# First channel product of six token groups as seven block products for eight, in a DeltaNet and low-rank mixer kernel

## The chip, the core and the metric

The kernel runs on one core of one Trainium2 chip. The metric is the device time of one execution in microseconds; the median of three runs of the kernel before is 591.05 us (590.74 to 592.5). The engines are called as in the profile: PE (TensorE matmuls; PEld is its weight loads), DVE (VectorE), ACT (ScalarE), POOL (GpSimd) and SP (SyncE, which here issues transfers).

## The reference

Four sequences of 768 tokens, eight heads of width 48. A delta-rule recurrence per head gives `x`, and a mixer follows. Its two channel products, `u @ w_ch1` (384 to 1536) and the product with `w_ch2` (1536 to 384), are most of the arithmetic.

```python
for t in range(S):                                   # 768 tokens
    kt, vt, bt = (k_n[:, :, t], v[:, :, t], beta[:, :, t, None])
    y[:, :, t] = np.einsum('bhd,bhde->bhe', q[:, :, t], state)
    v_old = np.einsum('bhde,bhd->bhe', state, kt)
    state = state + bt[:, :, :, None] * np.einsum('bhd,bhe->bhde', kt, vt - v_old)
...
xt = x.transpose(0, 2, 1)                            # x: (4, 768, 384)
h = xt @ U @ V                                       # over the tokens, rank 32
u = x + h.transpose(0, 2, 1)
ch = np.maximum(u @ w_ch1, 0.0) @ w_ch2
return (u + ch).astype(np.float32)
```

All matmuls are fp32. The weights arrive as 64-bit words and are converted on the chip.

## The kernel before

**Recurrence.** Each sequence is cut into 12 chunks of 64 tokens, in two units of six (`UC`); units are numbered 0 to 7. For each unit DVE inverts small triangular blocks by substitution (`blocks`, L790 and L796, a product and a subtraction for each of some 31 columns), PE joins the blocks with 32x32 products (L887 to L908), and `recur` walks the chunks: in the later units a step is a product with the state (L1066), a subtraction on DVE (`w`, L1078), a product (L1090), a copy on ACT (`z`, L1099), a product (L1135) and the new state on DVE (L1147, or L1149 for a sequence's first). Output products (L972, L986) go beside them. All of these use quarters of the array: four 64x64 (or 48x64) matmuls side by side, written in the planner as mode `"Q"`.

**Mixer.** A sequence has three groups of 256 tokens (`NG`), so there are twelve. `front` (L1469 to L1517) makes the transposed tokens `ut`. For groups 1 to 7 `wide` computes the first product as six pairs of output blocks (`PAIRS`, `channels`, L1580): for each pair six full 128x128 matmuls with 256 columns, three blocks of contraction for two blocks of outputs, into one PSUM bank, then one ReLU on ACT (L1545). A full matmul is mode `"F"`. A part whose key is in `PARTED` instead goes as 24 quarter matmuls (`crossed`, L393) over two banks, with a small ACT copy (`swap`, L402) between its halves. `add_up` (L1607) and `last_sum` (L1614) form sums of the hidden activations for the second product (`narrow`, L1695 in full and L393 in quarters), which is done as seven block products for eight over halves of its operands; `gather` (L1620) adds each result to `X`.

The last five groups (`EARLY` and `ordinal`) do the first product otherwise: `first_of` runs 15 block products for 18 (`CHAINS`, `products_of`, L1430), each of four full matmuls with 128 columns. A bank holds a running sum of products; after certain products it is drained: by an ACT copy or ReLU (L1406) where it is the first term of an output block, by a DVE addition or subtraction (L1412) where the block holds something already. `relu_of` (L1442) is the ReLU in SBUF. DVE makes the sums of weights and of tokens (`weight_sums`, `token_sums`, `sum_of`, L1350 and L1355).

**Weights.** `load_weights` brings slices into three places (`room` in `X`, `converted`, and a part of `hs`), and `convert` makes fp32 of them on DVE and ACT (L1229 to L1272), with `exponents` as a second buffer. After the last conversion, `converted` and `exponents` are not used again.

**Order.** The program is recorded through a small planner. Each part is a generator that asks for conditions (`need`) and engine slots (`op`). `ORDER` is a list, written out by hand for each of the five engines, of the parts' keys in the sequence in which their pieces are issued there; the planner follows it. A key such as `99.1` is the second child of part 99; before, `wide` of groups 1 to 12 has the keys 98 to 109 and `first_of` 93 to 97. So what an engine does next is fixed by the list, and it waits there if data are late. When PE goes from quarter to full pieces or back, the planner counts a turn (`TURN`). PSUM has eight banks: `pair` banks for the recurrence and the fronts, `mix` banks 0 and 1 for the mixer of groups 1 to 7, and four more for `CHAINS` once the recurrence is done (`reserve`).

Of the kernel before, what the change touches and what calls it, by code (L numbers as in the profile page):

```python
# [26 lines left out]
def kernel(  # L27
# [68 lines left out]
    def dve(n):  # L96
        return (n + 151) / 960.0
# [30 lines left out]
    def advance(i, value, at):  # L128
# [24 lines left out]
        4.12 32.1 4.13 4*2 4.13 4.14 4 4.15 4 4.14 4.15 79 32.0.0.0 81 32.1.0.0 81*2 40.0 82 98.0*2 39.0  # L153
        39.1 82 98.1 40.1 39.1.0.0 39.0.0.0 98.1 98.2 33.2*2 98.2 98.3*2 98.4 33.4*2 33.2 98.4 33.2 98.5
        33.4*2 33.2*2 98.5 98.7 83 33.2 33.4 33.2 33.4 98.7 33.4*2 98.8 5 5.0 5 40.1.0.0 5 98.8 5.1 5 98.9 5
        98.9 5 5.1 98.9 5 98.9 5.2 5 98.10 5 5.2 5.3 5 99.0 5 99.0 5 5.3 5.4 5 99.0 5 99.0 5.5 5 99.1*2 5
        5.4 99.1*2 5.5 40.0.0.0 5 83 99.2*2 99.3*2 99.4 48.0 99.4 41.2*2 47.0 99.7 47.1 47.0.0.0 47.1.0.0
        41.4*2 99.5*2 48.1 41.2 41.4*2 41.2 99.7 99.8 48.1.0.0 5 99.8 5.6 5 48.0.0.0 5 99.9 5 99.9 5.7 5*2
        99.9 5 5.6 99.9 5.8 5.7 5 99.10 5*2 100.0 5.9 5 100.0 5.8 5 100.0 5 100.0 5.9 5 5.10 5 100.1 5.11 5
        5.10 100.1 5 5.11 100.1*2 84 100.2*2 100.3*2 100.4*2 100.5 100.7 100.5 49.2*2 55.0.0.0 84 55.1.0.0  # L160
        100.7 100.8 49.2 49.4*2 49.2 100.8 84 100.9*2 6 85 100.9 6 100.9 56.0.0.0 56.1.0.0 6 100.10 49.4*2
        6.0 6 101.0*2 85 6.1 6 101.1*2 6 101.1 6 101.1 6.2 6 101.2*2 6.1 6 101.2*2 6 6.3 6.2 101.3 6 101.3 6
        6.4 6.3 6 101.4 6 101.4 6.5 6 101.4 6 101.4 6.4 6 6.5 101.5*2 101.7*2 57.2*2 57.4*2 86 57.4*2 57.2*2
        101.8*2 101.9*2 63.0.0.0 101.10 6 101.10 6 63.1.0.0 102.0*2 86 6.6 6 102.1*2 64.0.0.0 6 6.6 102.2 6
        102.2 6.7 6 102.2*2 6 6.7 102.3 6 102.3 6.8 6 102.3 6 102.3 6.9 6 102.4 6 102.4 6.8 6 102.4 6 102.4
        6.10 6 102.5*2 6.9 6.11 102.5 6 102.5 6.10 6 102.7 6.11 102.7 87 102.7*2 64.1.0.0 87 102.8*2 102.9*2
        102.10 71.0.0.0 103.0*2 71.1.0.0 103.1*2 103.2*2 103.3*2 65.4*2 65.2*2 103.4*2 72.1.0.0 65.2*2
        65.4*2 103.5*2 87 103.7 7 72.0.0.0 7 103.7 7 7.0 103.8*2 7.1 7 103.8*2 7 88 7 103.9*2 7 7.1 7.2 7
        103.10 7 7.2 104.0 7 104.0 7.3 7 104.0*2 7 7.3 7.4 104.1 7 104.1 7 104.1*2 7.5 7 7.4 104.2 7 104.2
        88 104.3*2 7 7.5 73.4*2 73.2*2 104.4*2 104.5 73.4*2 73.2*2 104.5 7 104.7 7 7.6 7 104.7 7 7.7 104.8  # L170
        7.6 7 104.8 7 104.8 7 104.8 7 7.7 7.8 7 104.9 7 7.8 7.9 7 104.9 7 89 7 104.10 7 7.9 7.10 7 7.11 7
        104.10 7 7.10 7.11 79 93.2 93.1 79 89 93.4 93.2 93.1 93.3 93.2 93.3 93.4 93.1 93.5 93.1 93.2 93.1
        94.2 94.3 93.1 90 94.3 94.4 94.2 90 94.1 105.3*2 94.1 94.2 90 94.1 94.5 94.1 94.4 94.2 105.4*2 105.5
        94.1 105.5 94.1 91 105.6 95.2 95.1 91 95.4 106.3 95.2 95.3 95.1 106.3 95.1 95.3 95.4 95.1 95.2
        106.4*2 95.5 95.1 106.5 95.2 96.3 95.1 106.5 96.1 106.6 92 96.4 96.2 96.1 92 96.2 96.4 96.1 96.2
        96.3 96.2 96.1 107.3*2 107.4*2 96.1 96.5 107.5*2 96.1 107.6 97.1 97.4 97.2 97.1 97.3 97.2 97.1
        108.3*2 97.1 97.3 97.2 97.5 108.4*2 97.1 97.2 108.5 97.1 108.5 108.6 97.4 109.3*2 109.4*2 109.5*2
        109.6
# [7 lines left out]
        31.0.0.0*2 31.1.0.0*2 4 33 4 30 4 78.25 4 33*2 4 78.25*2 33*2 78.26 32.0.0.0 78.26 81 33 78.26 81  # L186
        32.1.0.0*2 78.26 33 78.26 33 82 33*2 32.0.0.0 30 33*8 33.4 33.2 78.26.1*3 39.0.0.0 78.27 98.2.1*3
        39.1.0.0 78.26.1 39.0.0.0 30 78.27*4 39.1.0.0 33.2*3 33.4*2 78.27.1 33.4 41 98.5.1*2 78.27.1*2
        98.7.0 98.5.1 78.27.1 38 83 41 98.6 5 98.7.1 41*3 38 98.8.0 5 98.8.1 41*3 5 41 5 41*2 40.1.0.0
        98.9.0 41 98.9.1 5 40.1.0.0 41 98.10.0 5 41*2 5 41 5 41*2 5 41 5 41*15 41.2 5 99.2.1 40.0.0.0 99.2.1  # L190
        38 40.0.0.0 99.2.1 99.7.0 41.4 47.0.0.0*2 47.1.0.0*2 49 99.5.1*3 46 49*2 46 49*2 99.7.1 99.8.0 99.6
        5 48.1.0.0*2 99.8.1 49*2 48.0.0.0 5 48.0.0.0 49 5 49*2 5 49*2 5 99.9.0 49*2 99.9.1 49 99.10.0 5 49 5
        49*2 5 49 5 49*2 5 49 5 49*9 46 49*2 84 49 100.2.1*2 49.2 49.4 55.1.0 55.0.0 100.5.1*2 100.2.1
        100.5.1 100.7.0 84 55.1.0.0 55.0.0.0 55.1.0.0 100.7.1 55.0.0.0 100.6 57 100.8.0 54 100.8.1 56.0.0
        57*4 56.1.0 6 85 100.9.0 56.0.0.0 56.1.0.0 56.0.0.0 6 57 56.1.0.0 100.9.1 100.10.0 57*7 6 57 6 57*2
        6 57*2 6 57*3 101.2.1 57 6 57 6 57*2 6 57 6 57*5 6 54 57*3 57.2 101.2.1 101.7.0 57.4 101.2.1
        101.5.1*3 101.7.1 54 86 101.6 101.8.0 101.8.1 63.0.0 64.0.0 101.9.0 101.9.1 63.1.0 63.0.0.0 6
        63.0.0.0 101.10.1 101.10.0 64.1.0 63.1.0.0*2 65 62 65*2 6 65 64.0.0.0 62 6 64.0.0.0 65*2 6 65*2 6
        65*3 6 65 6 102.2.1 65 6 65 6 65*3 6 102.2.1*2 65 6 65 102.5.1*2 65 62 87 65 102.5.1 102.7.0 65*3
        102.7.1 65 102.8.0 65 102.6 102.8.1 87 65 102.9.0 65 71.0.0 65 102.9.1 102.10.0 64.1.0.0*2 71.1.0  # L200
        65*4 71.1.0.0 65 71.0.0.0 65.4 71.0.0.0 71.1.0.0 65.2 73 72.1.0 72.0.0 70 73*2 72.1.0.0 103.2.1 73
        72.1.0.0 73*3 103.2.1*2 73 103.7.0 103.5.1*2 72.0.0.0 73 7 103.5.1 103.7.1 73 72.0.0.0 7 73 103.6
        73*2 7 103.8.0 88 103.8.1 73 7 73*2 103.9.0 73*2 7 73 103.10.0 103.9.1 7 73*2 7 73*2 7 73*2 70 7
        73*3 7 73*6 73.2 73.4 7 70 80*3 104.2.1*2 80 104.2.1 104.5.1 7 80*2 93.0*2 104.5.1 7 104.7.0 104.5.1
        104.7.1 7 104.6 7*2 93.0 104.8.0 104.8.1 7 93.0 104.9.0 7 80 7 104.9.1 7 89 93.0 7*2 93.0*2 80
        93.0*2 80*2 93.0 80 104.10.0 80 93.2.1 94.0*3 80 93.1.1 93.0 80 93.3.1 93.2.2 93.1.2 93.1.3 104.10.1
        93.2.3 93.5.0 94.0 93.1.4 94.0*6 93.4.1 90 94.2.1 90 105.0*3 94.3.1 94.1.1 105.1 94.1.2 94.2.2
        105.1*2 105.3.1 105.3.0 95.0 94.1.3 95.0*4 94.5.0 94.2.3 95.0 105.4.0 94.0 105.2 94.4.1 95.0 105.4.1
        94.1.4 105.5.0 95.0*2 106.1*2 106.0 91 95.0 106.1 105.6.0 106.0 105.5.1 106.3.0 95.1.1 96.0*3 95.2.1
        106.0 95.0 95.1.2 95.4.1 106.3.1 106.2 96.0 95.3.1 95.1.3 106.4.0 95.2.2 96.0 106.4.1 96.0*3 95.5.0  # L210
        106.5.0 96.0*2 95.1.4 95.2.3 92 96.1.1 96.2.1 107.0 96.1.2 96.2.2 106.6.0 107.1*2 106.5.1 96.2.3
        97.0*4 107.1 107.0*2 107.3.0 97.0*2 107.3.1 96.3.1 97.0*3 107.4.0 96.0 96.1.3 96.4.1 107.2 107.4.1
        96.5.0 96.1.4 107.5.0 97.0 97.1.1 107.6.0 107.5.1 108.1 108.0 97.2.1 108.1 108.3.0 97.1.2 108.0
        108.3.1 108.1 97.0 108.0 97.3.1 108.2 108.4.0 97.1.3 97.5.0 97.2.2 97.1.4 97.2.3 108.5.0 108.4.1
        109.1*3 108.6.0 97.4.1 108.5.1 109.0 109.3.0 109.0*2 109.3.1 109.4.0 109.4.1 109.2 109.5.0 109.5.1
        109.6.0
# [8 lines left out]
        31.1.0.0 30 31.0.0.0 4.13*2 78.25.0 4.14*2 4.15*2 32.1.0 78.26.0 81 40.0.0 98.0.0 82 39.1.0 39.0.0  # L225
        39.0.0.0 40.1.0 98.1.0 33.2 98.2.0 78.27.0 39.1.0.0 39.0.0.0 33.4 98.3.0 39.1.0.0 33.1*2 98.4.0
        98.5.0 33.2 33.1*2 33.4 33.2 38 33.2 33.4*2 5 33.3 5.0*2 5 33.3*3 98.9 5.1*2 5*2 99.0 5.2*2 5.3 5
        5.3 99.0.0 99.1 5.4*2 5 99.1.0 5.5*2 99.2.0 83 48.0.0 99.4.0 99.3.0 41.2 41.1 47.0.0 47.1.0 47.0.0.0
        47.1.0.0 47.0.0.0 41.4 47.1.0.0 99.5.0 48.1.0 46 41.1*2 41.4 41.2 41.1 41.2 41.3 41.4 5 99.9 5
        41.3*3 5.6*2 5 5.7*2 5 100.0 5.8*2 100.0.0 5 5.9*2 5.10 100.1 5 5.10 5.11*2 100.1.0 100.2.0 100.3.0  # L230
        100.4.0 49.1*2 100.5.0 49.2 55.0.0.0 49.3 55.1.0.0 55.0.0.0 49.3*3 54 49.2*2 49.4 49.1*2 84 100.9
        55.1.0.0 6 6.0 49.4*2 6.0 6 101.0.0 85 101.1 6 101.1.0 101.2 6.1*2 101.2.0 6.2 6 6.2 101.3.0 6 6.3*2
# [1544 lines left out]
```

## Time and profile before

| what | value |
| --- | --- |
| median of three runs | 591.05 us |
| profiled execution | 589.15 us |
| its span, first to last instruction | 587.4 us |
| mean granted TensorE clock | 0.939 |
| DMA | 35.17 MB, 60 GB/s on average |
| L1580 (first product, full), 128x256 | 348 records, 81.8 us |
| L393 (both products, quarters) | 624 records of 128x256's form and 672 of 128x192's |
| L1430 (15 for 18), 128x128 | 600 records with L1430 in all |
| L790 and L796 (substitution on DVE) | 200 each, 63.7 and 64.6 us |
| L1545 (ReLU out of PSUM on ACT) | 42, 597 ns each |
| L1412 (DVE addition from PSUM) | 50, 684 ns each |
| L1442 (ReLU in SBUF on ACT) | 25, 625 ns each |

A row of the page gives for a group of instructions the line, the engine, the operation, the tiles and shapes, the count, the busy time and the mean length of one, then the engine's idle time before them and what ended it. An fp32 matmul leaves two records. The page's table of slices shows the busy share of each engine in 40 equal parts of the span in tenths. The table of stages gives, for a stretch of time, each engine's busy time with its number of instructions, the granted clock and the transfers.

### The profile page before, as it was taken

To read this page: it belongs to the slowest core of one execution; us is meant where nothing else is said; L and a number is where in the kernel's file an instruction comes from. 1 tells how busy PE (TensorE), PEld (TensorE's weight loads), DVE (VectorE), ACT (ScalarE), POOL (GpSimd) and SP (SyncE) were. 2 spreads that over 40 slices of the span, in tenths; PEclk is the share of its full clock that TensorE was granted. 3 is DMA by queue.
4 is the path that set the end of the run, shared out by engine and by line. 5 is a ranking of instruction groups with operands and counts; after the bars stand their busy time and mean duration, and the time that the engine had idled before them with its cause. 6 is when DMAs were issued, how large, how long until landed. Compare 5 with 4: busy or idle time off the path is not lost.

```text
span 587.4 us, 25542 instructions
## 1 busy us (share of the span) xinstructions
PE 545.3 (93%) x11460; PEld 491.1 (84%) x11460; DVE 456.2 (78%) x1086; ACT 227.3 (39%) x483; POOL 118.1 (20%) x205
## 2 busy tenths in 40 slices
PE   5697778799999999999999999999999999999997
PEld 4586677588888987997897798988889999999997
DVE  6898999999899898899878888888547574555552
ACT  4447476544433623344344305324423422131220
POOL 8132050311205304340252253301000000000000
PEclk9576666799999999999999999999999999999999
DMA  9634676652104314223212433200000000000013
GB/s 157 85 76 128 192 188 166 134 91 63 29 4 83 68 22 83 74 53 63 48 30 61 80 75 71 60 29 3 2 5 1 2 1 1 1 2 1 1 42 119
DMA packets 79213, 35.17 MB, mean 60 GB/s; under 512 B 65600, under 2 KB 76992, under 8 KB 79104
## 3 DMA queue, kind: packets, MB, share of 16 engines
q1 hardware_dynamic: 71200, 24.10, 18.9%
q0 software_dynamic: 6304, 9.15, 7.2%
q8 instruction: 90, 1.47, 1.0%
q10 hardware_dynamic: 1600, 0.30, 0.3%
q14 instruction: 19, 0.16, 0.1%
HBM read 28.80 MB, written 4.72 MB: 57 GB/s over the span
## 4 chain that ended last, share of the span: by engine, by line
PE 79%; DVE 7%; ACT 5%; DMA 4%; issue 3%; SPq 1%; POOL 1%; DVEq 0%; ACTq 0%; POOLq 0%
PE P L1695 24%; PE P L1580 12%; PE P L1430 12%; PE P L393 10%; PE P L704 3%; DMA wide<-in_moe_w_ch_dram 2%; PE P L668 2%; PE P L1066 2%; PE P L1090 1%; PE P L972 1%; PE P L1486 1%; PE P L986 1%; PE P L1135 1%; PE P L1514 1%; PE P L861 1%
## 5 line engine op out<-in xcount | busy, mean ns | idle before, releaser
L1695 PE MATMUL P<-w_sb,hs 128*128 128x192 f32 x480 | 84.2, 329 | 0.1
L1580 PE MATMUL P<-ut,w_sb 128*128 128x256 f32 x348 | 81.8, 386 | 0.1
L1695 PEld LDWEIGHTS P<-w_sb,hs 128*128 128x128 f32 x480 | 77.7, 190 | 1.3 <-issue 0.3
L1580 PEld LDWEIGHTS P<-ut,w_sb 128*128 128x128 f32 x348 | 64.1, 190 | 9.4 <-issue 0.6
L796 DVE TENSOR_TENSOR xt<-xt,prod 128x112 f32<-128x112 f32 (+21 forms) x200 | 64.6, 323 | 6.9
L790 DVE TENSOR_TENSOR prod<-gs,xt 128x112 f32<-128x112 f32 (+21 forms) x200 | 63.7, 319 | 3.9
L1620 DVE TENSOR_TENSOR X<-X,P 128x192 f32<-128x192 f32 x86 | 29.6, 349 | 36.1 <-PE P L1695 34.2
L1545 ACT ACTIVATE hs<-P 128x512 f32<-128x512 f32 x42 | 24.8, 597 | 62.1 <-PE P L1580 51.0
L393 PE MATMUL P<-ut,w_sb 64*64 64x256 f32 x624 | 43.0, 384 | 1.2 <-ACT hs L1545 0.9
L956 ACT COPY X<-P 64x192 f32<-64x192 f32 x96 | 30.0, 312 | 28.8 <-PE P L986 27.2
L704 PE MATMUL P<-slot 48*64 48x64 f32 x1536 | 33.5, 245 | 1.9 <-ACT slot L682 1.6
L704 PEld LDWEIGHTS P<-slot 48*64 48x64 f32 x1536 | 30.0, 157 | 6.1 <-ACT slot L682 2.5
L933 POOL MEMSET slot<- 32x384 f32 x32 | 13.4, 420 | 102.6 <-PE P L890 40.4
L1412 DVE TENSOR_TENSOR hs<-hs,P 128x512 f32<-128x512 f32 x30 | 20.1, 684 | 17.5 <-PE P L1430 9.2
L1695 PE MATMUL P<-w_sb,S 128*128 128x192 f32 x192 | 33.7, 330 | 0.0
L926 ACT COPY slot<-zz 32x384 f32<-32x384 f32 x64 | 32.3, 508 | 1.0
L1099 ACT COPY z<-P 128x192 f32<-128x192 f32 x36 | 11.5, 319 | 53.3 <-PE P L1090 46.4
L1695 PEld LDWEIGHTS P<-w_sb,S 128*128 128x128 f32 x192 | 31.1, 190 | 0.6 <-DVE xt L796 0.3
L548 POOL DMA_DIRECT2D slot<-in_k_dram x44 | 28.7, 657 | 12.3 <-PE P L1135 10.6
L668 PE MATMUL P<-ident,slot 128*128 128x128 f32 x108 | 20.0, 343 | 11.3 <-DMA slot<-in_k_dram 5.7
L1430 PE MATMUL P<-slot 128*128 128x128 f32 x240 | 29.7, 276 | 0.0
L1695 PE MATMUL P<-w_sb,slot 128*128 128x192 f32 x168 | 29.1, 327 | 0.0
(171 smaller groups left out, 1140.9 us busy)
## 6 DMA issues: line engine op xcount, KB each, us to landing
out_dram<-X SPq DMA_DIRECT2D x22, 192.0 KB, 2.0
X<-in_moe_w_ch_dram SPq DMA_DIRECT2D x10, 384.0 KB, 4.4
wide<-in_moe_w_ch_dram SPq DMA_DIRECT2D x10, 384.0 KB, 4.4
slot<-in_k_dram SPq DMA_DIRECT2D x48, 72.0 KB, 3.7
slot<-in_k_dram POOLq DMA_DIRECT2D x44, 72.0 KB, 3.1
slot<-in_v_dram SPq DMA_DIRECT2D x32, 72.0 KB, 3.7
slot<-in_v_dram POOLq DMA_DIRECT2D x32, 72.0 KB, 3.2
hs<-in_moe_w_ch_dram SPq DMA_DIRECT2D x4, 384.0 KB, 5.7
```

The source lines that it names most:

```text
L393: nc.tensor.matmul(to[half(g)], w[half(r), half(g)], x[half(r)], start=start, stop=stop, skip_group_check=True,)
L548: queue.dma_start(out=t[half(1 - g if name == "z" else g), :, to, 0:D], in_=src[b, 4 * g + s, hf * UC * L : (hf + 1) * UC * L, :].rearrang ...
L668: nc.tensor.transpose(p_t[:, c // 3, c % 3], t[:, c, 2 * j : 2 * j + 2].rearrange("p s d -> p (s d)"), ident,)
L704: nc.tensor.matmul(p_g[half(g ^ (par * i)), par, c], kq[rows, c, j, 0, half(g)], kq[rows, c, j, i, half(g)], start=True, stop=True,)
L790: nc.vector.tensor_tensor(out=prod, in0=gb[:, :, j : j + 1, j + 1 :].to_broadcast([128, split, m, w]), in1=xb[:, :, 0:m, j : j + 1].to_bro ...
L796: nc.vector.tensor_tensor(out=xb[:, :, 0:m, j + 1 :], in0=xb[:, :, 0:m, j + 1 :], in1=prod, op=ALU.subtract,)
L926: nc.scalar.copy(pg[quarter(i), :, at, :, a : a + BK], cut(zc, h)[quarter(i)].rearrange("p r (c j) t -> p r c j t", j=2),)
L956: nc.scalar.copy(x[half(c % 2), c // 2, 4 * D * g : 4 * D * (g + 1)].rearrange("p (j r d) -> p r j d", r=2, d=D), states(p_y)[half(g)],)
L1430: nc.tensor.matmul(bank[:, q], w_block(w)[:, q // 2, 128 * (q % 2) : 128 * (q % 2) + 128], token(b, i, t), start=c == 0 and q == 0, stop=True,
L1580: nc.tensor.matmul(p_f[:, x], w(x, t), ut[:, t], start=(t == 0), stop=(t == KT - 1))
L1620: nc.vector.tensor_tensor(out=to, in0=to, in1=p, op=ALU.add)
L1695: nc.tensor.matmul(to, of[0], of[1], start=of[2], stop=of[3], skip_group_check=True)
```

## The change

Groups 2 to 7 (`SEVENS`) no longer run pairs 0 to 3 of the first product through `channels`. Those four pairs are two thirds of the outputs. Over two thirds of the contraction they are taken as a product of 2x2 blocks by 2x2 blocks (two thirds of the outputs in two halves, two of the three contraction blocks, two halves of the tokens) in seven block products instead of eight; the remaining third of the contraction is added in four plain block products. So there are eleven block products (`SEVEN`, 44 full matmuls with 128 columns) where there were 24 matmuls with 256 columns. Pairs 4 and 5 stay in `channels`.

- `four_sums` makes four sums of weight blocks on DVE, once, in `converted` and `exponents`, after the last weight is converted.
- `four_tokens` makes four sums of token blocks on DVE for each group, in part of `S2`.
- `sevens` runs four chains of block products in `mix` banks 0 and 1; where a step has an outcome, the bank is drained: by an ACT copy (first term of an output block) or a DVE addition (second term). `positive` is the ReLU in SBUF that follows the second term.
- `all_read` and `both_halves` pass on the conditions that `channels` and `relu` passed on before.
- `PARTED` has ten keys for 25, and the five lists of `ORDER` are new from the first sequence's mixer on; the parts' keys from 80 on move up by one, since `four_sums` is a part.

Per group this adds on DVE four additions from PSUM (128x512) and four of 128x128, and on ACT four copies out of PSUM and four ReLUs in SBUF for four ReLUs out of PSUM.

```diff
     PARTED = set("""
-        81 86 19.0 40.0 98.9 99.0 99.1 99.9 100.0 100.1 100.9 101.1 101.2 101.4 101.10 102.2 102.3 102.4
-        102.5 102.7 103.8 104.0 104.1 104.8 104.10
+        82 84 86 19.0 40.0 47.0 48.0 100.15 103.8 105.16
...
                 out=to, in0=a, in1=c, op=ALU.add if s == t else ALU.subtract
             )
 
+    SEVENS = {(0, 1), (0, 2), (1, 0), (1, 1), (1, 2), (2, 0)}
+
+    def four(z):
+        return (converted[:, 512 * z :] if z < 3 else exponents).bitcast(FP32)[:, 0:512].rearrange(
+            "p (y x) -> p y x", y=2
+        )
+
+    def four_sums():
+        yield need(("weights", W2 + 5))
+        for z, (a, c) in enumerate(((3, 4), (13, 0), (0, 3), (1, 14))):
+            yield op("dve", dve(512), port=True)
+            a, c = (four(x - 13) if x >= 13 else w_block(x) for x in (a, c))
+            nc.vector.tensor_tensor(out=four(z), in0=a, in1=c, op=ALU.subtract if z else ALU.add)
+            emitted(("four", z), 0.1)
+
     def weight_sums():
 
         yield need(("weights", W2 - 1), *freed(N - 2))
         yield op("pe", 0.0, take=("pair", 1))
         free["mix"].update({4: state["now"], 5: state["now"]})
 
+    SEVEN = (
+        ((0, 0, (0, 0, 0)), (14, 7, (0, 1, 1)), (15, 8, (1, 0, 0)), (5, 5, (1, 1, 1))),
+        ((13, 6, (1, 1, 0)), (16, 3, ()), (2, 5, (0, 1, 0))),
+        ((1, 2, ()), (2, 4, (0, 0, 1))),
+        ((4, 9, ()), (5, 4, (1, 0, 1))),
+    )
+
     def wide(b, i):
         yield need(("front", b, i), cleared(b, i), *freed(N - 1) * (ordinal(b, i) > 0 and ordinal(b, i) % 2))
         x = X[:, b % 2]
 
         def channels(e):
             y, fs = e, PAIRS[e]
-            yield need(("weights", 2 + y), *[("channels", b, i, y - 1)] * (y > 0))
+            yield need(("weights", 2 + y), *[("channels", b, i, y - 1)] * (y > (4 if (b, i) in SEVENS else 0)))
 
             def w(x, t):
                 return w1_sb[:, y, 256 * t + 128 * x :][:, 0:128]
                         )
                 ms = (m,)
             emitted(("channels", b, i, y))
-            if y == len(PAIRS) - 1:
+            if y == len(PAIRS) - 1 and (b, i) not in SEVENS:
                 emitted(("wide", b, i))
             begin(relu(fs, ms, p_f), 3)
-            if y % 3 == 2:
+            if y % 3 == 2 and (b, i) not in SEVENS:
                 begin(add_up(y // 3 * 3, PAIRS[y - 2 : y + 1]), 4)
+
+        def of_tokens(z):
+            return S2[:, z - 6] if z > 5 else ut[:, z // 2, 128 * (z % 2) : 128 * (z % 2) + 128]
+
+        def four_tokens():
+            yield need(("front", b, i), cleared(b, i), ("weights", W2 + 5))
+            for z, (a, c) in enumerate(((1, 0), (3, 6), (3, 1), (2, 7))):
+                yield op("dve", dve(128), port=True)
+                nc.vector.tensor_tensor(
+                    out=of_tokens(6 + z), in0=of_tokens(a), in1=of_tokens(c), op=ALU.subtract
+                )
+                emitted(("four token", b, i, z), 0.1)
+
+        def outcome(n, m):
+            h = hs[:, :, 128 * m : 128 * m + 128].rearrange("p (k f) n -> p k f n", k=2)
+            return h.rearrange("p k f n -> p f k n")[:, 2:4] if n else h[:, :, 0:2]
+
+        def sevens(e):
+            y = min(e, 1)
+            yield need(("front", b, i), *[("sevens", b, i, e - 1)] * (e > 1))
+            bank = mixed(y).rearrange("p (q n) -> p q n", q=4)
+            steps = SEVEN[e]
+
+            def drained(c, n, m, k):
+                if k:
+                    yield need(("sevenheld", b, i, n, m))
+                    yield op("dve", dve(512), give=[("mix", y)] if c == len(steps) - 1 else ())
+                else:
+                    yield op("act", act(512), give=[("mix", y)] if c == len(steps) - 1 else ())
+                to, p = outcome(n, m), bank.rearrange("p (a x) n -> p a x n", a=2)
+                if k:
+                    nc.vector.tensor_tensor(out=to, in0=to, in1=p, op=ALU.add)
+                    begin(positive(n, m), 3)
+                else:
+                    nc.scalar.copy(to, p)
+                    emitted(("sevenheld", b, i, n, m), 0.06)
+                emitted(("sevenout", b, i, e, c), 0.1)
+
+            for c, (w, z, out_of) in enumerate(steps):
+                yield need(
+                    *[("sevenout", b, i, e, c - 1)] * (c > 0 and bool(steps[c - 1][2])),
+                    *[("four", w - 13)] * (w > 12), *[("four token", b, i, z - 6)] * (z > 5),
+                )
+                yield op("pe", 0.893, "F", take=None if c else ("mix", y), words=16)
+                wb = four(w - 13) if w > 12 else w_block(w)
+                for u in range(4):
+                    nc.tensor.matmul(
+                        bank[:, u], wb[:, u // 2, 128 * (u % 2) : 128 * (u % 2) + 128], of_tokens(z),
+                        start=c == 0 and u == 0, stop=True, skip_group_check=True,
+                    )
+                if out_of:
+                    begin(drained(c, *out_of), 3)
+            emitted(("sevens", b, i, e))
+
+        def positive(n, m):
+            yield op("act", act(512))
+            nc.scalar.activation(outcome(n, m), outcome(n, m), ACTF.Relu)
+            emitted(("positive", b, i, n, m), 0.06)
+
+        def both_halves(n):
+            yield need(*[("positive", b, i, n, m) for m in range(2)])
+            for fs in PAIRS[2 * n : 2 * n + 2]:
+                emitted(("h", b, i, fs))
+
+        def all_read():
+            yield need(*[("sevens", b, i, e) for e in range(4)], *[("channels", b, i, y) for y in (4, 5)])
+            emitted(("wide", b, i))
 
         def part(k, m, f0, n=3):
             return hs[:, k * HF + f0 : k * HF + f0 + n, 128 * m : 128 * m + 128]
         if ordinal(b, i) >= 0:
             for f0 in range(0, HF, 3):
                 begin(add_up(f0, ()), 4)
+        elif (b, i) in SEVENS:
+            begin(four_tokens(), 3)
+            begin(all_read(), 95)
+            for n in range(2):
+                begin(both_halves(n), 95)
+            for e in range(4):
+                begin(sevens(e), 95)
+            for e in range(4, len(PAIRS)):
+                begin(channels(e), 95)
+            for e in range(2):
+                begin(add_up(3 * e, PAIRS[3 * e : 3 * e + 3]), 4)
         else:
             for e in range(len(PAIRS)):
                 begin(channels(e), 95)
                         begin(load(n, name, some), FIRST.get((name, n), 20 + 4 * n + y))
         begin(load_weights(), 40)
         begin(reserve(), 0)
+        begin(four_sums(), 96)
         begin(weight_sums(), 97)
         for b in range(B):
             for i in range(NG):
```

More of the change, by code (lines that the diff above doesn't have):

```diff
@@ L157 @@
[L157 to L161, printed above, removed]
@@ L179 @@
+        98.1 109.3 98.1 98.2 109.4*2 98.2 98.5 109.5 98.1 109.5 98.1 109.6 110.3*2 110.4*2 110.5*2 110.6
         """,
@@ new lines @@
+        5 41 40.1.0.0 5 41 99.8.0 41*4 5 41 80 99.8.1 84 41*2 99.9.0 5 41 38 41 5 38 80 99.9.1 5 99.10.0
+        100.0 41 100.0 5 41 5 80*2 41 100.0 5 41*2 5 41*3 100.0 100.4.1 5 41*2 100.6.0 41*2 100.4.3 41
+        40.0.0.0 41*4 100.7.0 41 40.0.0.0 41*2 41.4 47.0.0.0 41.2 47.1.0.0*2 47.0.0.0 100.10 49 100.10*2
+        100.11*3 100.13.0 46 49*2 100.12 100.13.1 48.0.0.0 49 5 48.0.0.0 49*3 5 48.1.0.0 100.14.0 49
+        48.1.0.0 100.14.1 5 49*3 5 49 5 49*4 5 100.15.0 46 49 5 49 101.0 49 100.15.1 5 49 5 49*3 5 101.0
@@ L217 @@
+        110.3.1 110.4.0 110.4.1 110.2 110.5.0 110.5.1 110.6.0
         """,
@@ new lines @@
+        63.1.0.0 103.5.0 6 57.3 62 57.3 87 103.5.1 103.4.0 6 6.6*2 6.7 103.4.2 6.7 6 6.8 6 103.4.1.0
+        103.7.0.0 6.8 6.9 6 103.8 6.9 103.6.0.0 6 103.8.0 103.4.3.0 6.11 6.10*2 6.11 103.9.0 71.0.0.0
+        104.5.0 104.4.0 71.0.0.0 104.5.1 104.4.2 71.1.0.0 65.1*2 65.2 71.1.0.0 65.1 104.6.0.0 65.4 70 65.1
+        104.7.0.0 65.2 104.4.3.0 65.3 104.8.0 65.4*2 65.2 65.3 104.9.0 88 104.4.1.0 65.3*2 7*2 7.0*2 7 7.1*2
+        105.5.0 7.2*2 7 105.4.0 105.5.1 7.3*2 105.4.2 7 105.8.0 7 105.4.3.0 7.5 7.4*2 105.7.0.0 7.5
@@ L245 @@
+        98.2.0 97.4.1.0 98.4.0 98.3.0 98.4.0 98.4.1.0 98.1.3.0 98.2.3.0 98.1.4.0 98.5.0.0 98.1.5
         """,
```

161 lines of the change are left out of this document (78 added, 83 removed).

## The prediction

> **What bounds the kernel now.** I read the page's busy shares first, then the busy time of each engine by stage, then what PE waits for in the long middle stage, then the chain of waits for the price of single pieces of PE work.
>
> The page's first two parts say which engines can matter at all:
>
> ```profile
> PE 545.3 (93%) x11460; PEld 491.1 (84%) x11460; DVE 456.2 (78%) x1086; ACT 227.3 (39%) x483; POOL 118.1 (20%) x205
> ...
> PE   5697778799999999999999999999999999999997
> PEld 4586677588888987997897798988889999999997
> DVE  6898999999899898899878888888547574555552
> ```
>
> PE is full from about the tenth of the 40 slices on, and DVE is nearly full beside it until slice 28, where the recurrences end. I cut the span at three points of the recurrence: 109.6 us (the last state update of sequence 0, L1147), 157.6 us (the first one of sequence 1, L1149) and 437.9 us (the last one of sequence 3). Columns are the stage, its length, the busy time of each engine with its instructions, the granted clock, the DMA share and GB/s:
>
> ```profile
> 109.60:157.60 48.00, 45.81 (x1219) 38.65 (x1223) 44.09 (x92) 20.86 (x40) 15.16 (x25) 0.93 0.45 90
> 157.60:437.90 280.30, 274.41 (x6586) 238.03 (x6578) 233.62 (x586) 107.38 (x259) 71.25 (x121) 1.00 0.23 48
> 437.90:587.40 149.50, 146.06 (x1220) 143.12 (x1220) 80.79 (x185) 35.43 (x64) 0.00 (x0) 1.00 0.05 17
> ```
>
> The middle stage has PE at 98% and DVE at 83%. The third has PE alone. So the time is PE's work plus small waits; the first 109.6 us have the same order on PE in both programs. The waits that the trace names for PE in the middle stage are small:
>
> ```profile
> PE P L393 <- ACT hs L1545: 1.1, 4, 0.4
> PE P L1135 <- ACT z L1099: 0.9, 3, 0.5
> PE P L1066 <- DVE s L1147: 0.6, 1, 0.6
> ```
>
> All seven rows of that answer sum to 4.0 us. The change's groups run in the middle stage, so what it is worth is decided there. The chain of waits gives the prices (start, length, piece; two trace records make one matmul):
>
> ```profile
> 303.43 0.86 PE P L704 x48
> 304.29 0.98 PE P L393 x24
> ...
> 306.70 0.71 PE P L704 x48
> 307.41 2.79 PE P L1580 x12
> ...
> 404.51 2.59 PE P L1580 x12
> ...
> 480.00 0.89 PE P L1430 x8
> ```
>
> A channel pair in full 128x128 matmuls (L1580, 12 records) takes 2.59 us after another full piece and 2.79 after a quartered one: 0.20 to turn. The same 48 records of L704 take 0.86 after a full piece and 0.71 after a quartered one: 0.15 to turn back. A round trip costs 0.35 us. A block product of four matmuls with 128 columns (L1430, 8 records) takes 0.89.
>
> **The change part by part, on PE.** The instruction orders of the two programs give the counts.
>
> - First product. Of 42 channel pairs, 29 ran full and 13 quartered; 17 and 1 are left, and 66 block products (11 in each of six groups) replace 24 pairs. 12 full pairs less: 12 x 2.59 = -31.1. 12 quartered less: one half is 0.88 + 0.45 by the starts of its two pieces, so 2.66 a pair: -31.9. 66 x 0.89 = +58.7. Sum -4.3.
> - Other forms. 11 of the second products (264 quarter matmuls) run full: 12 records take 1.95 against 1.98 for two L393 pieces of 0.99: -0.3. Three transposes of 6 full matmuls (1.31, by L668 in the chain) become 24 quarter ones (the 0.72 of L704's 24, the nearest row): -1.8. The 17 small copies that stood between the halves of quartered pairs (L402) go; 0.5 us of weight-load waits name them: -0.5.
> - Turns. A block product exists only in full form, the recurrence only in quarters. Changes between full and quartered pieces rise from 78 to 141 (other changes stay at 58): 31.5 round trips x 0.35 = +11.0.
>
> PE's sum is +4.1 us: the seven-for-eight saving is smaller than the turns that the blocks force when they are dealt out between steps of the recurrence. By the three recurrence points, the same tally puts about -2.7 before 157.6 and the rest, nearly +7, after it. In the stage to 157.6 DVE is busy 44.1 of 48.0 us and gets no less to do, and its weight conversions wait for DMA; PE's saving there can come out whole or not at all. I take half: PE's net is +5.5, between +4.1 and +6.8.
>
> One rule bears on the turns. The Trainium skill, "TensorEngine Tiling (Array Packing)", section "Key Properties", says that changing the tiling mode, not merely the tile, drains TensorE. By that rule all 31.5 trips are paid, also where PE then waits for data; the trace's 0.20 and 0.15 agree where PE didn't wait, and the sum would be the same +11.0; the last rival below is what it would be if waits swallowed them.
>
> **On DVE.** Added: 24 additions from PSUM (128x512; L1412 is the same operation, 0.684), 24 token sums (128x128; L1355, 0.284) and four weight sums (128x512 in SBUF; L1355's row with w_sb, 0.686): 16.4 + 6.8 + 2.7 = 25.9 us. Back to back, DVE instructions overlap: between the two points their lengths add up to 252.6 us and the busy time is 233.6, a factor 0.925. So +24.0, and DVE goes from 83% to 92% of the stage. It is hidden as long as DVE's own idle time there (46.7 us) can take it. The idle time is mostly DVE standing in its order for PE results (L1620 for L1695 9.6 us, L1147 for L1135 6.5), so not all can be filled.
>
> The Trainium skill, "VectorE: DVE Perf Modes", section "The DRAIN you can't avoid", has it that the next operation doesn't start until the pipe is empty. By that it would be the full 25.9 us; the trace shows the overlap just given, so 24.0 stays.
>
> **On ACT.** 24 copies out of PSUM (0.597 by L1406) stand for 24 ReLUs of the same size (L1545, 0.597), and 24 ReLUs in SBUF come on top (L1442, 0.625): +15.0, less 17 copies of 0.160 (-2.7). ACT is busy 38% of the middle stage; +12.3 makes 43%. Nothing, unless a ReLU stands ahead of the recurrence's z copy (L1099): then that step is 0.6 us late and PE with it.
>
> **New waits.** Two banks carry the chains of block products, and a product that adds to a drained bank waits for the ACT copy (0.60) or the DVE addition (0.68). Queued behind it on PE are the recurrence's next pieces. With the banks taken in turn, the other bank's product (0.89) covers the drain. Low bound: none, as in the last stage, where L1430 pieces stand at 0.89 apart nearly always. High bound: each of the 24 DVE drains finds one other DVE operation of about 0.35 (the mean of the L790 and L796 rows is 0.32) ahead of it: 8.4 us. The last stage has the same operations in the same chains, so its rows are the nearest and pull toward none; but its DVE is 54% busy against 92% here, so not none: I take 2.0. For other stalls I count nothing either way.
>
> **Sum.** +5.5 + 2.0 = +7.5 us. The profiled execution took 589.15 us (span 587.4 and 1.7 around it), so it would be 596.6; the median shown is 1.9 above it, so **598.5 us** for a median. Likeliest case's own range: 594 (PE's +4.1, no new waits, a little filled) to 604 (+6.8 and +8.4 less a part).
>
> **Rivals.**
>
> - *DVE takes the pace.* DVE keeps the waits that it has, because PE's results come no sooner, and the 24.0 us come on top where it is already late: the substitution (L790, L796) of the next unit ends late, the block inverses (L887 to L908) start late, and the recurrence after them. For it: DVE at 92%, and the 46.7 us of idle time are scattered (the longest named wait is 2.6 us). Against it: much of the idle time is just waiting for PE. If two thirds isn't absorbed, +16: 607 us.
> - *Turns lost in waits (faster).* In the recurrence's bursts PE waits anyway for DVE's w and s and ACT's z, and a turn inside such a wait costs nothing. In the middle stage the prices of all pieces and turns sum to 265.5 of 280.3 us; the 32x32 products (L887 to L908) take 6.4 us more by their starts than I priced them, which leaves 8.4 us of waits. If the turns fill all of that: -6.9 + 11.0 - 8.4 = -4.3, so 586.8 us. It decides from 6 us of hidden turns on. Against it: the chain shows the 0.20 and 0.15 wherever PE is full, and PE is at 98%.
> - *No change.* About 4 us of turns are hidden, no new waits: 591 us.
> - *The saving isn't there.* If a block product with operands in the conversion buffers cost more than 0.89, each 0.1 would add 6.6 us; L1430 has the same price from three different places (276 to 278 ns a record), so this stays inside the upper range.
>
> **Chances.** Forecast 0.58, DVE takes the pace 0.18, no change 0.11, turns lost in waits 0.13. A measurement of this kernel tells apart 0.3%, or 1.8 us: faster means under 589.3, slower over 592.8. The forecast and DVE's rival are slower: 0.58 + 0.18, less 0.02 for the forecast's lower edge, 0.74; same 0.12; faster 0.14. The range reaches from 589.5 to 607.5: it takes in the no-change case and the DVE rival's value, and leaves out most of the faster one and the DVE rival's upper half, about 2 in 10.
>
> **What would show it.** In the changed kernel's profile: 8 records of the new block product 0.89 apart in full runs, and 0.2 more after a quartered piece; the middle stage, to the last L1147, longer by 6 to 9 us with PE still at 97% or more; the last stage unchanged at 149.5; DVE near 257 us of it busy; no new row of PE waits over 3 us. It would be wrong if PE's busy share in the middle stage fell to 94% with waits for DVE (the DVE rival), or if that stage got shorter (turns lost in waits).

## The result, and the profile after

| what | before | changed |
| --- | --- | --- |
| median of three runs | 591.05 us | 609.15 us (606.98 to 610.64) |
| ratio of the runs, 95% interval | | 1.0296 (1.0239 to 1.0352) |
| profiled execution, its span | 589.15, 587.4 us | 609.15, 607.4 us |

The changed kernel is slower by 18.1 us; 7.5 were forecast, and the time lies above the predicted range (589.5 to 607.5). In the page after, PE's share has fallen by a point and DVE's stands where it was:

```profile
PE 556.5 (92%) x10998; PEld 510.0 (84%) x10998; DVE 476.4 (78%) x1137; ACT 237.8 (39%) x490; POOL 118.1 (19%) x205
...
PE   5696778699999989999989999999999999999997
...
DVE  6899998998898998898877998899848556644642
```

The stages, cut at the same three state updates (now L1149, and L1151 for a sequence's first), in the same columns as before:

```profile
111.30:159.90 48.60, 44.61 (x1141) 38.31 (x1142) 44.23 (x96) 20.70 (x38) 13.93 (x23) 0.87 0.43 84
159.90:457.60 297.70, 285.83 (x6189) 256.92 (x6187) 252.78 (x633) 118.27 (x267) 70.51 (x120) 1.00 0.22 45
457.60:607.40 149.80, 145.89 (x1220) 142.68 (x1220) 81.62 (x186) 35.29 (x64) 0.00 (x0) 1.00 0.05 17
```

Of the 20.0 us between the spans, the middle stage has 17.4 (297.7 less 280.3), the second 0.6 and the last 0.3. The first 109.6 us have 1.7 more here, but PE's order there is that of before, and this stretch came to 111 to 113 us in the profiles of kernels below whose order there is also that of before; this part isn't laid to the change. So 18.3 us are to be explained.

In the middle stage PE is busy 11.4 us more and idle 6.0 us more (11.9 against 5.9). Its named waits there, in us in total, times and longest, first of the changed kernel:

```profile
PE P L1068 <- DVE s L1149: 2.2, 4, 0.7
PE P L1137 <- ACT z L1101: 1.5, 5, 0.4
PE P L1092 <- DVE w L1080: 1.3, 5, 0.3
PE P L974 <- DVE s L1149: 1.3, 2, 0.7
PE P L988 <- ACT z L1101: 1.1, 3, 0.5
```

Two more rows name no releaser ("issue"):

```profile
PE P L910 <- issue: 1.0, 1, 1.0
PE P L1137 <- issue: 0.7, 1, 0.7
```

Before, beside the rows of 0.9 and 0.6 that the prediction shows for `z` and `s`, there are these:

```profile
PE P L986 <- ACT z L1099: 0.5, 1, 0.5
PE P L972 <- DVE s L1147: 0.4, 2, 0.2
PE P L1090 <- DVE w L1078: 0.2, 1, 0.2
```

All rows of the answer after sum to 10.7 us in 25 waits, against 4.0 in 13 before. No row is long. The five rows for the state `s`, for `w` and for `z` are waits at the recurrence's own hops; a hop is the way from one piece of the recurrence on PE, over DVE or ACT, to the next piece that needs its result. They sum to 7.4 us, against 2.6 before: 4.8 of the 6.7 us that were added. Why PE stood in the two "issue" waits is open. The new block product's line isn't among the waiting ones.

The chain of waits gives the price of the block product (L1660; 8 records are one):

```profile
230.03 1.10 PE P L1660 x8
...
232.41 1.98 PE P L1660 x16
...
237.44 3.77 PE P L1660 x32
```

All three stand behind a quartered piece: 1.10 for one, 1.98 for two, 3.77 for four. So each further one costs 0.88 to 0.90, and the first 0.2 more. The price of the work was right. What was wrong has to lie in how often PE turns, in what a turn costs, and in the hops. PE's forms in the traces confirm how often: in the middle stage the changes between full and quartered pieces go from 52 to 115, so all of the 31.5 more round trips lie there, and those between full pieces and 32x32 products from 18 to 20.

### The profile page after: what moved, and what is told of

Read it like the earlier page. It is cut to its first block, busy times and chain, and to the rows that moved or that the text cites. A ratio compares the mean times of both kernels' runs of the same rounds, so it can differ in the third digit from the quotient of the medians.

```text
span 607.4 us, 24682 instructions
## 1 busy us (share of the span) xinstructions
PE 556.5 (92%) x10998; PEld 510.0 (84%) x10998; DVE 476.4 (78%) x1137; ACT 237.8 (39%) x490; POOL 118.1 (19%) x205
## 4 chain that ended last, share of the span: by engine, by line
PE 77%; DVE 11%; ACT 4%; issue 3%; DMA 3%; POOL 1%; SPq 0%; DVEq 0%; ACTq 0%; POOLq 0%
PE P L1786 26%; PE P L1447 11%; PE P L1660 10%; PE P L1604 7%; PE P L706 3%; PE P L1137 2%; DMA wide<-in_moe_w_ch_dram 2%; PE P L1092 2%; PE P L1068 2%; PE P L974 2%; PE P L670 2%; PE P L988 1%; PE P L1503 1%; DVE prod L792 1%; PE P L863 1%
## 5 line engine op out<-in xcount | busy, mean ns | idle before, releaser
L1786 PE MATMUL P<-w_sb,hs 128*128 128x192 f32 x564 | 99.1, 329 | 0.5 <-DVE X L1711 0.5
L1786 PEld LDWEIGHTS P<-w_sb,hs 128*128 128x128 f32 x564 | 91.3, 190 | 2.2 <-issue 1.4
L1604 PE MATMUL P<-ut,w_sb 128*128 128x256 f32 x204 | 49.1, 389 | 0.2 <-DVE hs L1645 0.2
L1786 PE MATMUL P<-w_sb,S 128*128 128x192 f32 x240 | 42.9, 331 | 0.0
L1604 PEld LDWEIGHTS P<-ut,w_sb 128*128 128x128 f32 x204 | 37.6, 192 | 5.7 <-DVE hs L1645 0.6
L1786 PEld LDWEIGHTS P<-w_sb,S 128*128 128x128 f32 x240 | 38.7, 190 | 1.0 <-DVE prod L792 0.3
L1660 PE MATMUL P<-ut,w_sb 128*128 128x128 f32 x288 | 39.2, 282 | 0.0
L1660 PEld LDWEIGHTS P<-ut,w_sb 128*128 128x128 f32 x288 | 34.7, 192 | 1.1 <-issue 0.3
L1429 DVE TENSOR_TENSOR hs<-hs,P 128x512 f32<-128x512 f32 x30 | 20.1, 684 | 14.6 <-PE P L1447 14.4
L550 POOL DMA_DIRECT2D slot<-in_v_dram x32 | 20.8, 658 | 53.9 <-PE P L670 35.2
```

Of the source, the lines that this page charges most:

```text
L550: queue.dma_start(out=t[half(1 - g if name == "z" else g), :, to, 0:D], in_=src[b, 4 * g + s, hf * UC * L : (hf + 1) * UC * L, :].rearrang ...
L1429: nc.vector.tensor_tensor(out=to, in0=to, in1=p, op=ALU.add if s > 0 else ALU.subtract)
L1604: nc.tensor.matmul(p_f[:, x], w(x, t), ut[:, t], start=(t == 0), stop=(t == KT - 1))
L1660: nc.tensor.matmul(bank[:, u], wb[:, u // 2, 128 * (u % 2) : 128 * (u % 2) + 128], of_tokens(z), start=c == 0 and u == 0, stop=True, skip_ ...
L1786: nc.tensor.matmul(to, of[0], of[1], start=of[2], stop=of[3], skip_group_check=True)
```

## Experiments

Four theories stood at first. *DVE*: its 24 us of added work set the pace. *Turns*: a change between full and quartered pieces costs more than I took. *Lumps*: full pieces can only be issued whole, so they no longer cover the recurrence's hops as halves of quartered parts did. *Drains*: new waits of the block products for their banks. In the diffs `+` and `-` stand against the kernel that the text names; each run has the kernel before beside it on the same chip (its medians there are 591.18 to 593.56 us), and the ratios are to that.

**Without the added DVE work** (changed kernel; the sums of tokens and the additions from PSUM are left out).

```diff
-                nc.vector.tensor_tensor(
-                    out=of_tokens(6 + z), in0=of_tokens(a), in1=of_tokens(c), op=ALU.subtract
-                )
...
-                    nc.vector.tensor_tensor(out=to, in0=to, in1=p, op=ALU.add)
```

> The changed kernel without the 24 token differences and the 24 additions from PSUM that the block products brought to DVE (their outcomes are then only the first terms); every other instruction and every order stays. 23.2 us of DVE lengths less, PE's pieces and turns the same. If DVE's added work is what makes the recurrence late, most of the 18 us come back: 594 to 599 us. If PE's turns and the way the full pieces are dealt out cost the time, little comes back: 605 to 609 us.

Measured: 609.89 us, ratio to before 1.0276 (1.0247 to 1.0305). The stage, and two of its waits:

```profile
161.30:459.10 297.80, 286.96 (x6189) 258.22 (x6187) 235.24 (x585) 118.29 (x267) 70.66 (x120) 0.99 0.23 45
```

```profile
PE P L1068 <- DVE s L1149: 2.2, 4, 0.7
PE P L1137 <- ACT z L1101: 1.5, 5, 0.4
```

DVE is busy 17.5 us less (235.2 for 252.8), the stage is as long, and the rows for `s`, `w` and `z` are the same to a tenth. The DVE theory falls: PE doesn't wait for `s` because the added work makes DVE late.

**Three of four matmuls of each block product** (changed kernel; a quarter of each block product is left out).

```diff
-                for u in range(4):
+                for u in range(3):
```

> The changed kernel with three of the four matmuls of each block product (a quarter of their outputs is left out). 66 matmuls less at 0.22 us, 14.7 us of PE work less, the same turns, the same work on DVE and ACT. If PE sets the pace, 594 to 597 us. If DVE does, the time hardly moves: 604 to 609 us.

Measured: 602.09 us, 1.0145 (1.0123 to 1.0166).

```profile
160.10:449.50 289.40, 275.27 (x6057) 244.02 (x6055) 251.14 (x634) 118.35 (x267) 70.66 (x120) 0.99 0.24 46
```

66 matmuls of 0.223 are 14.7 us of PE work; the stage lost 8.3 and PE's busy time 10.6. The 2.3 us between these two went into waits: they come to 12.6 us, and the row of `w` (L1092) grew from 1.3 to 2.0. Where the other 4 us of PE's work stayed is open. The time lies between the two that were expected: PE's work is worth its time only in part. That the block products also cover hops would explain the added waits, but this run doesn't isolate it.

**Turns alone, where nothing waits** (before; in the last stage, whose PE order is nearly one long run of full pieces, a quarter matmul of 64 columns is put ahead of each of the 35 second products, which makes 34 more round trips; it also changes what is summed in their banks, so the output of these groups is another).

```diff
+                    if ordinal(b, i) >= 0:
+                        nc.tensor.matmul(
+                            mixed(x)[half(0), 256:320], w2_sb[half(0), 0, 0, 0:L], S1[half(0), 0, 0:L],
+                            start=True, stop=True, skip_group_check=True,
+                        )
                     for f in range(HF):
```

> The kernel before with one small quarter matmul (64 columns, unused result) ahead of each second product of the last five groups: 34 more round trips between full and quartered pieces in the stage where PE is alone, nothing else. By my price of 0.35 us and 0.03 for the matmul 34 x 0.38 = 13 us: 604 us. If a turn costs less in a full stream, 591 to 597; if it costs more than I priced, over 607.

Measured: 608.87 us, 1.0265 (1.0242 to 1.0287). The last stage, and PE's timeline in it (start, length, engine, line, tiles, forms, records):

```profile
441.00:605.80 164.80, 161.34 (x1290) 150.50 (x1290) 81.10 (x185) 35.42 (x64) 0.00 (x0) 1.00 0.04 15
```

```profile
538.34 0.33 PE L1694 MATMUL P<-S,w_sb 64*64 64x64 f32 x2
538.59 2.22 PE L1700 MATMUL P<-w_sb,hs 128*128 128x192 f32 x12
540.74 0.33 PE L1694 MATMUL P<-S,w_sb 64*64 64x64 f32 x2
540.99 1.24 PE L1700 MATMUL P<-w_sb,S 128*128 128x192 f32 x6
```

From one small matmul to the next it is 2.40 us, for a piece that takes 1.95 in a run; 0.25 lies between the small one's start and the full piece's. The stage grew by 15.3 us (164.8 less 149.5), 0.45 for each of 34 trips. The small matmul itself is some 0.03 of that, an estimate (48 records of L704 take 0.71, so two take 0.03). No run puts a small full matmul there instead, so it isn't shown that all of it is the change of form and none the interruption as such; the next run changes the form without small matmuls. My price of 0.35 had come from the turn back into a long quartered piece, and was too low.

**The same 19 parts in full instead of quartered** (before; nothing of the change is in it, but 19 of the parts that are quartered before are taken out of `PARTED`, and `thin` shortens their places in the order to match).

```diff
+    FULL = "98.9 99.0 99.1 99.9 100.0 100.1 100.9 101.1 101.2 101.4 102.2 102.3 102.4 102.5 102.7 103.8 104.0 104.1 104.8"
+    PARTED -= set(FULL.split())
...
-        queues, heads = {e: queue(of) for e, of in ORDER.items()}, dict.fromkeys(ORDER, 0)
+        queues, heads = {e: queue(thin(of, e)) for e, of in ORDER.items()}, dict.fromkeys(ORDER, 0)
```

> The kernel before with 19 quartered parts of its first and second products (13 channel pairs, 6 pairs of second products) run as full matmuls where their halves stood: 36 more round trips, almost as many as the change's 31.5, without any added work on DVE. By the prices: 36 x 0.35 = 12.6, less 1.7 for the cheaper form and the dropped copies: 602 us. If turns vanish in waits: 588 to 593 us. If dealing full pieces between the steps of the recurrence makes new waits too, over 605 us; then these waits need no DVE work to arise.

Measured: 610.0 us, 1.0276 (1.0253 to 1.0300).

```profile
159.80:456.80 297.00, 285.74 (x5682) 245.44 (x5674) 234.28 (x585) 104.12 (x240) 71.27 (x121) 1.00 0.23 45
```

```profile
PE P L1149 <- ACT z L1113: 3.5, 12, 0.5
PE P L1104 <- DVE w L1092: 2.2, 7, 0.5
PE P L1080 <- DVE s L1161: 2.1, 4, 0.6
```

Without one block product and with none of the added work on DVE, the stage is nearly as long as the changed kernel's (297.0 for 297.7), and the same three hops wait. (Its lines for `z`, `w` and the state are L1149, L1104 and L1080.) This kernel has both suspects in it, 36 more round trips and the lumps, so the next two take them apart.

**Lumps alone** (before; the same 19 parts stay quartered, but their second and fourth pieces are issued right behind the first and third; work and turns are unchanged).

```diff
+    def lumped(of):
+        seen, out = {}, []
+        for key in of:
+            seen[key] = seen.get(key, 0) + (key in LUMP)
+            if seen[key] not in (2, 4):
+                out += [key] * (1 + (key in LUMP))
+        return out
...
-        queues, heads = {e: queue(of) for e, of in ORDER.items()}, dict.fromkeys(ORDER, 0)
+        queues, heads = {e: lumped(queue(of)) if e == "pe" else queue(of) for e, of in ORDER.items()}, dict.fromkeys(ORDER, 0)
```

> The kernel before with the same 19 quartered parts, still quartered, but the two pieces of each half (0.88 and 0.45 us, or 0.99 and 0.99) issued one behind the other where the first stood: same work, same number of turns as before, but a step of the recurrence that had the second piece as its cover now has none. By the order, steps with less than 0.75 us between two of the recurrence's pieces go from 32 to 38 and what they lack from 7.6 to 18.0 us. If lumps between the recurrence's steps make waits, 599 to 603 us on this chip's 593.5; if only turns cost, 593 to 595.

Measured: 600.7 us, 1.0145 (1.0111 to 1.0179): some 9 us, and the middle stage is 288.2, 7.9 more than before, of which 6.0 are idle time of PE.

```profile
160.90:449.10 288.20, 276.29 (x6582) 240.53 (x6571) 233.69 (x585) 106.35 (x259) 71.29 (x121) 1.00 0.23 46
```

```profile
PE P L1145 <- ACT z L1109: 2.3, 8, 0.5
PE P L1100 <- DVE w L1088: 2.2, 7, 0.5
PE P L1076 <- DVE s L1157: 2.0, 4, 0.6
```

How that comes about is seen in the timeline. First before, one step of the recurrence (L1066 is the product with the state, L1090 the one with `w`, L1135 the one with `z`; L393 is half of a quartered piece of the second product, 24 records):

```profile
208.76 0.36 PE L1135 MATMUL P<-z,slot 64*48 64x48 f32 x16
208.93 1.17 PE L393 MATMUL P<-w_sb,hs 64*64 64x192 f32 x24
209.95 0.45 PE L1066 MATMUL P<-s,slot 48*64 48x48 f32 x16
210.22 1.17 PE L393 MATMUL P<-w_sb,hs 64*64 64x192 f32 x24
211.21 0.40 PE L972 MATMUL P<-s,slot 48*64 48x48 f32 x16
211.43 0.42 PE L1090 MATMUL P<-w,slot 64*64 64x48 f32 x16
212.32 0.40 PE L1135 MATMUL P<-z,slot 64*48 64x48 f32 x16 [0.48 <-ACT z L1099]
```

Then the lumped kernel at the same place (here L1145, L403, L1076, L982, L1100):

```profile
213.76 0.36 PE L1145 MATMUL P<-z,slot 64*48 64x48 f32 x16
213.94 2.15 PE L403 MATMUL P<-w_sb,hs 64*64 64x192 f32 x48
215.90 0.40 PE L1076 MATMUL P<-s,slot 48*64 48x48 f32 x16
216.12 0.41 PE L982 MATMUL P<-s,slot 48*64 48x48 f32 x16
216.78 0.45 PE L1100 MATMUL P<-w,slot 64*64 64x48 f32 x16 [0.24 <-DVE w L1088]
217.71 0.40 PE L1145 MATMUL P<-z,slot 64*48 64x48 f32 x16 [0.48 <-ACT z L1109]
```

Before, each of the two hops, to the new state and to `w`, has one half of 1.0 us under it. Lumped, the first hop has 2.0 us, though DVE has the new state (L1157) done 0.8 us after L1145, and the hop to `w` has only the 0.22 of L982: PE waits 0.24, the brackets say for `w`. The hop to `z` has nothing under it in either, and PE waits the same 0.48. The work is the same; only its dealing out differs. The stage's named waits come to 10.7 us, as in the changed kernel; the rows for `s`, `w` and `z` sum to 9.0.

**Turns alone, covers kept** (before; in each half of the 19 parts one full matmul of 64 columns into an unused part of a bank is put between the first and the second block).

```diff
+        def alone_full(w, x):
+            nc.tensor.matmul(
+                mixed(0)[:, 256:320], w, x, start=False, stop=True, skip_group_check=True
+            )
+
...
+                        if t == 0:
+                            alone_full(w(0, 0), ut[:, 0, 0:L])
...
+                        if f == 0:
+                            alone_full(w2_sb[:, 0, 0, 0:128], ut[:, 0, 0:L])
```

> The kernel before with one full matmul of 64 columns (result unused) inside each half of the 19 quartered parts: 38 round trips more, in the same places as those of the run with full pieces, while every step of the recurrence keeps its cover. 38 matmuls x 0.05 = 2 us and 38 trips: at my price of 0.35 us 608.5, at the 0.43 of the last stage 611.5. If turns vanish in the recurrence's waits, under 601.

Measured: 611.04 us, 1.0322 (1.0283 to 1.0361).

```profile
161.00:460.60 299.60, 293.67 (x6658) 244.50 (x6650) 234.21 (x585) 107.31 (x259) 71.27 (x121) 1.00 0.22 45
```

```profile
PE P L393 <- ACT hs L1550: 1.1, 4, 0.4
PE P L1135 <- ACT z L1099: 0.9, 3, 0.5
PE P L1066 <- DVE s L1147: 0.6, 1, 0.6
```

The waits are those of before to the tenth, and the stage grew by 19.3 us, all of it PE's busy time: 0.51 for each of 38 trips with the small matmul in it. The small matmul's own price isn't measured; by proportion its 64 columns are some 0.12 (0.223 for a matmul of 128 columns, less the 0.102 between that and the 0.325 of one of 192), which leaves an estimate of 0.39 for a trip, near the 0.42 to 0.45 of the last stage. The rule that the prediction took from the Trainium skill, "TensorEngine Tiling (Array Packing)", "Key Properties", agrees: the 38 trips were paid among the recurrence's steps too.

**Without the drains** (changed kernel; the copies and additions that drain the banks are left out, so the block products' sums go nowhere).

```diff
-                    nc.vector.tensor_tensor(out=to, in0=to, in1=p, op=ALU.add)
...
-                    nc.scalar.copy(to, p)
```

> The changed kernel without the 24 copies and 24 additions that drain the block products' banks (so the first product of two thirds of the outputs of these groups is left out of the result): no block product waits for a drain any more; PE's pieces and turns stay. If the drains hold PE up, under 606 us; if not, 609 to 611.

Measured: 608.75 us, 1.0296 (1.0255 to 1.0338).

```profile
159.20:454.60 295.40, 285.22 (x6189) 256.69 (x6187) 239.67 (x609) 105.21 (x243) 70.66 (x120) 1.00 0.23 45
```

DVE and ACT have 13 us less to do each, and the run's ratio is that of the changed kernel, with an interval of some 2.5 us either way. In this one profile the stage is 2.3 us shorter, 1.7 of it PE's idle time, of which 1.0 is the "issue" wait at L910 that is gone. So the drains aren't the main cause; whether they cost nothing or about 2 us is open.

**One group alone** (before, with the change's functions for group 7 only, on the last two thirds of the outputs; four weight sums and four token sums with them). Three orders were run.

```diff
+    SEVENS = {(2, 0)}
```

The first order was found anew, so that other parts moved too:

> The change for one group alone, number 7, and for its pairs 2 to 5, which the kernel before runs in full between other full pieces: 11 block products in these places, 0.57 us of PE work less, four changes between forms more (0.7 us), DVE and ACT as in the change, for one group of six. The steps of the recurrence keep their cover (they lack 7.5 us against 7.6). If the block products themselves, their drains or sums cost what the change lost, a sixth of it, 3 us: 596.5. If dealing them out costs it, 593 to 595.

Measured: 593.81 us, 1.0031 (1.0009 to 1.0053). 2.6 us of it lie in the second stage (50.7 us), which group 7 doesn't touch: inconclusive. In the next one the weight sums stand later on DVE:

> The run with one group, its four weight sums (4 x 0.68 us on DVE) moved out of the stage before the first state update of sequence 1 into four places of the middle stage. In that run this stage was 2.6 us longer than before, which is what the sums cost there if DVE sets its pace. If so, the stage comes back to 48 to 49 us, the middle stage has room for them, and the whole is 0 to 1 us over the kernel before (ratio 0.999 to 1.002). If PE set that stage's pace, the stage was longer by chance and the ratio stays near 1.003.

Measured: 595.62 us, 1.0051 (1.0027 to 1.0076). The expectation failed: the second stage is still 50.4, so the place of the weight sums wasn't its cause. What was is open; these two orders differ from that of before elsewhere too. The third keeps the other parts in the order of before on every engine (the four weight sums alone come between them on DVE), and puts the block products where the group's own pairs stood:

> Again the change for group 7 alone, on its pairs 2 to 5, with every other part in the order of the kernel before (the two runs before had other parts moved too, and with them the stage to the first state update of sequence 1). 11 block products in full runs, 0.57 us of PE work less, one change between forms more, four weight sums on DVE. If block products, drains and sums cost by themselves what the change lost, a sixth of 18 us: ratio 1.005. If dealing them out between the recurrence's steps costs it: 0.998 to 1.002.

Measured: 592.43 us, 1.0017 (0.9996 to 1.0038).

```profile
160.00:441.10 281.10, 274.17 (x6626) 239.40 (x6617) 238.38 (x597) 109.74 (x263) 71.43 (x121) 1.00 0.23 48
```

The middle stage is 0.7 us longer than before. A sixth of the loss would be 3 us, or 1.005, which the interval leaves out. PE's busy time is 0.2 us less and its idle time 1.0 more, and one new wait, for the substitution on DVE, is 0.9 of that. So block products, sums and drains by themselves don't make up the loss; up to 2.2 us for a group (1.0038) isn't excluded. None of these runs is faster than before.

## Why the prediction was right or wrong

The direction was right, for part of the reason: the seven-for-eight saving is smaller than the turns it brings. The size was not. By its own steps:

- *"For other stalls I count nothing either way."* This is the step that failed. The halves of quartered parts that stood in the hops were counted as PE work and as turns, and their other job, to cover the hops, was not. The named waits of the middle stage rose by 6.7 us (10.7 less 4.0), and 4.8 of it stands in the rows for `s`, `w` and `z`. The lumped kernel shows that such a loss needs no turn and no DVE work: 9 us from issuing the same halves in pairs. A count in the traces says the same. Take a hop as short of cover where less than 0.75 us of other PE work stands between the two pieces (the longest single wait for `s`, `w` or `z` after is 0.7). Of 96 hops in the middle stage 29 were short before, lacking 6.0 us in all; 37 are in the changed kernel, lacking 13.0, and 37 in the lumped one, lacking 16.1. Such a count needs only the instruction orders and the prices of the pieces, so it can be made ahead of a run.
- *Turns, "31.5 round trips x 0.35 = +11.0"*: the mechanism right, the size too low. Measured by themselves they cost 0.42 to 0.45 in the last stage and, by estimate, 0.39 in the middle one; at 0.39 to 0.45 the term is 12.3 to 14.2, one to three us more. My 0.15 for the way back was read off a piece of 24 matmuls.
- *"-2.7 before 157.6", taken half*: none came out. PE's busy time in the second stage fell by 1.2 us (45.81 to 44.61), but the stage is 48.6 for 48.0, and PE's longest wait there, for DVE's `X`, went from 1.3 to 2.6 us. That term was off by some 2 us, but the runs with the order of before in this stage took 47.6 to 49.3 us there, so one profile can't settle it.
- *New waits for drains, "I take 2.0"*: not settled. No wait of L1660 is in the profile, and the run without drains has the ratio of the changed kernel; but its middle stage is 2.3 us shorter. The size taken, 2.0, is as possible as the low bound.
- *The block product at 0.89, and 0.2 more after a quartered piece*: right (0.88 to 0.90; 1.10).
- *DVE's work is hidden*: right, and more clearly than I gave it credit for. Its busy time came near the sum (252.8 for 257), 85% of a longer stage, and taking 17.5 us of it out left the stage at 297.8. The rival "DVE takes the pace" named a time close to the measured one (607 for 609.15), by luck: its cause isn't there.
- *Signs.* The last stage unchanged: right (149.8). The middle one longer by 6 to 9 us with PE at 97% or more: wrong, 17.4 and 96%. No row of new waits over 3 us: true, and it misled, since the added waits are many rows of 2.2 us at most.

The middle stage's 17.4 us add up as 6.7 of waits, 32.5 more round trips (31.5 of them between full and quartered pieces, one between full pieces and 32x32 products) at 0.39 to 0.45 (12.7 to 14.6), and about 4 less of work by the prediction's own prices: 15.4 to 17.3. This split is worked out, not isolated: the parts don't simply add. Lumps alone cost 7.9 us of the stage and trips alone 19.3 with their small matmuls, and the kernel with the parts in full, which has both, 16.7. There the work is 1.7 us less by the prices and the waits 6.3 more, so its 36 trips come to (16.7 + 1.7 - 6.3) / 36 = 0.34 each. If that is less than a trip alone, a turn that falls into a wait is partly free, as the rival "turns lost in waits" said; the prices are too rough to show it. The rival was outweighed, because the same edit made the waits.

## What to carry to other kernels

Filler work between dependent steps has two values, its own time and the hop that it hides; before replacing it, count for each hop how much independent work stands in it after the change, since pieces that can't be split leave some hops overfull and others bare. Price a change of array mode from a short piece between two long ones, both ways, and multiply by the count of changes in the new order. A busy engine whose added work looks like the obvious culprit is tested cheaply by taking that work out.

## What was not expected of the hardware

- A change from full 128x128 matmuls to quarter ones and back costs 0.42 to 0.45 us around a single small matmul (15.3 us for 34 trips), so some 0.2 each way; around a long quartered piece I had read 0.35. 38 trips with all named waits unchanged, small matmuls included, cost about as much as the whole change (19.3 us of the stage against 17.4).
- 48 more DVE operations, 17.5 us of busy time on an engine at 85%, cost nothing that can be measured (297.8 for 297.7 us of the stage without them), while the lumped kernel, with PE at 96%, lost 9 us to where PE's pieces stood.
- The first stretch, to the first sequence's last state update, took 109.6 to 113.0 us in executions whose PE order there is the same: a spread of 3 us that a single profile doesn't show.
